# Block-sparse attention with a soft mixture of experts: probabilities turned on the vector engine, values kept on chip, all engines ordered by a planner

## The chip, the cores and the metric

The kernel runs on one core of one Trainium2 chip. The metric is the time of one execution in microseconds (us), the median of several runs; lower is better. The engines are named as in the profile: PE multiplies matrices, DVE is the vector engine, ACT the scalar engine, POOL the general engine, SP issues DMAs. Everything is float32.

## The reference, cut to what matters

```python
# q, k, v: [4 batches, 8 heads, 768 positions, 64]; blocks of 32 positions, 24 of them
scores = q @ k^T / 8
mask = |blk_i - blk_j| <= 1, or blk_i in (0, 23), or blk_j in (0, 23), or blk_j one of 3 sampled for blk_i
attn = softmax(where(mask, scores, -1e9));  x = (attn @ v) as [3072 tokens, 512]
logits = x @ phi                       # [3072, 32]: 8 experts of 4 slots each
d = softmax over tokens(logits);  c = softmax over slots(logits)
slot_input = d^T @ x                   # [32, 512]
slot_out[e] = relu(slot_input[e] @ w1[e]) @ w2[e]      # w1 [8, 512, 1024], w2 [8, 1024, 512]
out = c @ slot_out                     # [3072, 512]
```

A block of queries between 1 and 22 therefore meets eight blocks of keys: the first and the last, its own with its two neighbours, and three sampled ones (a sampled block that is there already counts once). Blocks 0 and 23 of the queries meet all keys.

## The kernel before, in words

The work of a batch is cut into units. A *sparse* unit is one block of 32 queries with all eight heads (88 of them in the four batches); a *dense* unit is a pair of heads for the query blocks 0 and 23 together (16 of them).

For a sparse unit POOL and ACT first gather 256 keys from `ktile` into a stage `kst` (`stage_k`: the fixed blocks on POOL in lines 190 and 193, the three sampled ones on ACT in line 199, with block numbers read into registers). The values of the unit are loaded from DRAM for that unit alone into a stage `vst` (`stage_v`: plain DMAs on SP and an indirect DMA issued by POOL in line 219). `do_qk` (line 306) multiplies queries with keys: a product takes the 128 rows of a pair of heads, with zeros in the queries of DRAM where the other head stands, and 64 columns of the array. `do_soft` takes the maximum on DVE (line 322) and the exponential on ACT (line 325). `do_tr` turns the probabilities with four products against an identity on PE (line 354) and copies them out of PSUM on DVE or ACT in turn (lines 335 and 337). `av_half` (line 391) multiplies with the values for four units at a time, one head to a product, 65 columns wide (the 65th holds ones and gives the sum); lines 398 to 400 divide. Dense units do the same in lines 298, 313, 319, 345 and 371.

A *tile* is 128 tokens. `moe_front` takes each of the 24 tiles through PE turns (413), logits (458, 465, 466), a running maximum, an exponential (473), and a sum over tokens into `sacc` (497, 500). After the last tile the experts run: `ffn1` (714), `ffn2` (722), and `combine` (814), which writes the result in two column halves with `store`. The expert weights come in 64 pieces of 512 KB (`load_w`, line 80); 29 have places of their own and are issued during the attention, 15 more take the place of attention buffers as these come free, and the rest follow as pieces are used up.

PE and DVE follow the order in which the program is written: the main loop runs two or three units ahead with the first products, and fixed offsets (`EOFF`) place the steps of `moe_front`. The other engines are ordered by the framework. SP carries all plain DMAs in one queue.

Of the kernel before, what the change touches and what calls it, by code (L numbers as in the profile page):

```python
# [25 lines left out]
NE, SE, FF = 8, 4, 1024  # L26
NT = S // P
VW = H * (D + 1)
VROWS = S + BLK
# [3 lines left out]
# attention: buffers, and the order of the dense (D) and first sparse (S) units of a batch  # L33
NKST, NV, NQ = 3, 8, 3
PB, PTB, XB = 4, 4, 2
SB, TB = 3, 3
VORD = [3, 2, 1, 0, 7, 6, 5, 4]
ORDER0 = "DDSDDSS"
ORDER = "DSDDDSS"
KSTEP, VLOOK, VMOST, EARLY = 5, 7, 2, 4  # L40
EVPAT = "AD"
# half steps after a tile of tokens at which the parts of its slot input come, and for the last tiles
EOFF = [3, 6, 8, 9, 11, 15]
EOFFL = [[3, 7, 9, 10, 12, 13], [3, 6, 8, 9, 11, 13]]
# experts: w2 in CS column parts, weights in pieces of WP, NPRE of them loaded during the attention
# [7 lines left out]
NPRE, NLA, NLB = 29, 3, 12  # L53
W0, W1 = 3, 3
# [3 lines left out]
MAN = {mybir.EngineType.PE, mybir.EngineType.DVE}  # L58
TMAN = MAN | {mybir.EngineType.Activation}


@with_exitstack
def attn_moe_kernel(ctx, tc, qT, kT, vtab, sampled, phi, w1, w2, out):
# [4 lines left out]
    wpre = ctx.enter_context(tc.tile_pool(name="wpre", bufs=NPRE))  # L68
    pw = ctx.enter_context(tc.tile_pool(name="pw", bufs=2))

    wsrc = [w1[e, hf] for hf in range(2) for e in range(NE)]
    wsrc += [w2[s_, g] for s_ in range(CS) for g in range(NE)]
    # the weights come in pieces of [P, WP]
# [3 lines left out]
    def load_w(m, pool):  # L77
        t = pool.tile([P, WP], F32, name=f"w{m}", tag="w")
        n, j = m // PW, m % PW
        SP.dma_start(out=t, in_=wsrc[n].rearrange("p c f -> p (c f)")[:, j * WP:(j + 1) * WP])  # L80
        wtile[m] = t.rearrange("p (c f) -> p c f", f=512 if n < 2 * NE else CW)

# [14 lines left out]
    sacc = const.tile([P, P], F32, name="sacc")  # L97
    ssum = const.tile([P, 1], F32, name="ssum")

# [1 line left out]
    NG = 96  # L101
    sreg = const.tile([1, NB, NR], I32, name="sreg")
    gidx = const.tile([NG, B, NB], I32, name="gidx")

    scr = pw.tile([P, DM], F32, tag="x", name="scr", bufs=XB)
    sraw = scr[0:NG, 0:NB * NR * 2].bitcast(I32).rearrange("p (i j w) -> p i j w", i=NB, j=NR)

    def index_load():
        SP.dma_start(
            out=sraw.rearrange("p i j w -> p (i j w)"),  # L110
            in_=sampled.bitcast(I32).rearrange("i j -> (i j)").partition_broadcast(NG),
        )
        DVE.tensor_copy(out=sreg, in_=sraw[0:1, :, :, 0])

    def index_math():
        o = NB * NR * 2
        rf = scr[0:NG, o:o + NB * NR].rearrange("p (i j) -> p i j", i=NB)
        DVE.tensor_copy(out=rf, in_=sraw[:, :, :, 0])
        o += NB * NR
        own, dup, tmp, iot, pm = (scr[0:NG, o + k * NB:o + (k + 1) * NB] for k in range(5))  # L120
        for j in range(NR):
            s_ = slice(32 * j, 32 * j + 32)
            DVE.tensor_copy(out=own[s_], in_=rf[s_, :, j])
            POOL.iota(iot[s_], pattern=[[1, NB]], base=0, channel_multiplier=0,
                      allow_small_or_imprecise_dtypes=True)
            POOL.iota(pm[s_], pattern=[[0, NB]], base=0, channel_multiplier=1,
                      allow_small_or_imprecise_dtypes=True)
# [7 lines left out]
        for j in range(1, NR):  # L135
            s_ = slice(32 * j, 32 * j + 32)
            for k in range(j):
                DVE.tensor_tensor(out=tmp[s_], in0=own[s_], in1=rf[s_, :, k], op=ALU.is_equal)
                DVE.tensor_tensor(out=dup[s_], in0=dup[s_], in1=tmp[s_], op=ALU.max)
        DVE.tensor_scalar(out=own, in0=own, scalar1=float(BLK), scalar2=None, op0=ALU.mult)  # L140
        DVE.tensor_scalar(out=tmp, in0=own, scalar1=-1.0, scalar2=float(S), op0=ALU.mult, op1=ALU.add)
        DVE.tensor_tensor(out=tmp, in0=tmp, in1=dup, op=ALU.mult)
        DVE.tensor_tensor(out=own, in0=own, in1=tmp, op=ALU.add)
        DVE.tensor_tensor(out=own, in0=own, in1=pm, op=ALU.add)
        for b in range(B):
            DVE.tensor_scalar(out=gidx[:, b, :], in0=own, scalar1=float(b * VROWS), scalar2=None,
                              op0=ALU.add)

    # ================= attention =================
# [3 lines left out]
    pk = att.enter_context(tc.tile_pool(name="pk", bufs=1))  # L153
    pst = att.enter_context(tc.tile_pool(name="pst", bufs=1))

    ktile = pk.tile([P, NP, S], F32, name="ktile")
    # but for the first, in the order in which the end of the attention frees them, the last first
    kst = [pst.tile([P, NP, 256], F32, name="kst0")]
    vst = {n: pst.tile([P, 2, VW], F32, name=f"vst{n}") for n in VORD}
    kst += [pst.tile([P, NP, 256], F32, name=f"kst{n}") for n in range(1, NKST)]  # L160
    qc = [pst.tile([P, NP, 2, 2 * BLK], F32, name=f"qc{n}") for n in range(NQ)]

    vflat = vtab.rearrange("b s w -> (b s) w")

    def load_k(b):
        for p in range(NP):
            SP.dma_start(out=ktile[:, p, :], in_=kT[b, p])

    def load_q(b, c):
        SP.dma_start(out=qc[(b * (NB // 2) + c) % NQ], in_=qT[b, c])  # L170

    def q_of(b, i):
        c = (i + 1) // 2
        return qc[(b * (NB // 2) + c) % NQ][:, :, (i + 1) % 2, :]

    # running counters of the rotating stages
    nsp = [0]      # K stages filled
    vfree = list(range(NV))
    vown = {}
    kfresh = {}    # stage -> batch whose global keys it holds  # L180
    vfresh = {}

    def stage_k(b, i):
        n = nsp[0] % NKST
        nsp[0] += 1
        st = kst[n]
        kv = ktile
        if kfresh.get(n) != b:
            kfresh[n] = b
            POOL.tensor_scalar(out=st.rearrange("p c (g s) -> p c g s", g=2)[:, :, :, 0:BLK],  # L190
                               in0=kv.rearrange("p c (g s) -> p c g s", g=NB)[:, :, 0:NB:NB - 1, :],
                               scalar1=SCALE, scalar2=1.0, op0=ALU.mult, op1=ALU.mult)
        POOL.tensor_scalar(out=st[:, :, BLK:P], in0=kv[:, :, (i - 1) * BLK:(i + 2) * BLK],  # L193
                           scalar1=SCALE, scalar2=1.0, op0=ALU.mult, op1=ALU.mult)
        _, vals = nc.values_load_multi_w_load_instructions(
            sreg[0:1, i, :], engines=[mybir.EngineType.Activation], min_val=0, max_val=NB - 1,
            skip_runtime_bounds_check_because="block numbers lie in range by the definition of the input")
        for j in range(NR):
            ACT.activation(out=st[:, :, 160 + BLK * j:192 + BLK * j],  # L199
                           in_=kv[:, :, ds(vals[j] * BLK, BLK)], func=AF.Copy, scale=SCALE)  # L200
        return st
# [77 lines left out]
    def pump_v(lim, most=99):  # L279
        while vnext[0] < min(lim, len(units)) and most > 0:  # L280
# [7 lines left out]
            else:  # L288
                if not vfree:
                    return  # L290
# [615 lines left out]
```

## Time and profile before

| | |
|---|---|
| median of 3 runs | 391.88 us (389.75 to 396.16) |
| profiled execution, first to last instruction | 410.4 us (no other time of this execution is given) |
| PE, DVE, ACT, POOL busy | 353.6, 220.0, 209.9, 142.3 us |
| moved by DMA | 105.56 MB, 257 GB/s over the span |

The profiled execution is longer than the timed ones by 18.5 us; its durations are those of that one execution. "Busy" counts the time from the start of an instruction to its end, and neighbours overlap; the time that an instruction adds to a row of like ones is therefore its distance to the next start. An instruction on PE is one of two passes of a float32 product; a turn has one.

### The profile page before, as it was taken

How to read it: one execution, taken by the hardware profiler on the slowest of the kernel's cores; microseconds unless marked ns; L12 is line 12 of the kernel's file. 1: busy time of each engine (PE TensorE's matmuls, PEld its weight loads, DVE VectorE, ACT ScalarE, POOL GpSimd, SP SyncE). 2: the span in 40 equal slices, each digit the busy share in tenths (PEclk: the TensorE clock that was granted, in tenths of full speed). 3: DMA queues.
4: the chain of work that ended last, by engine and by line, in shares of the span. 5: the costliest groups of instructions: out<-in, count | busy, mean ns of one | idle time of the engine just before them, and what ended most of it. 6: DMA issues, size and time to landing. Idle time of an engine off the chain costs nothing.

```text
span 410.4 us, 14102 instructions
## 1 busy us (share of the span) xinstructions
PE 353.6 (86%) x5525; PEld 228.1 (56%) x5525; DVE 220.0 (54%) x618; ACT 209.9 (51%) x689; POOL 142.3 (35%) x216
## 2 busy tenths in 40 slices
PE   5788988799899867998999698989989899799970
PEld 2456655467566544665665465657556556435550
DVE  3655635466455535676565356756556687501350
ACT  1655756466457625672766276638556563310350
POOL 1625425432153544234445244333453243120000
PEclk9999999899899989999999799999999899999995
DMA  7977999989859979999599759965965499899978
GB/s 242 299 221 224 312 291 246 287 272 314 214 153 286 264 237 312 292 274 286 140 271 274 244 164 277 309 173 147 265 162 138 124 242 396 308 357 410 360 248 250
DMA packets 47841, 105.56 MB, mean 257 GB/s; under 512 B 6976, under 2 KB 13856, under 8 KB 47776
## 3 DMA queue, kind: packets, MB, share of 16 engines
q1 hardware_dynamic: 42144, 87.08, 68.5%
q0 software_dynamic: 5632, 17.58, 16.4%
q8 instruction: 44, 0.72, 0.8%
q14 instruction: 21, 0.17, 0.1%
HBM read 98.34 MB, written 6.29 MB: 255 GB/s over the span
## 4 chain that ended last, share of the span: by engine, by line
PE 81%; issue 6%; DVE 3%; DMA 3%; SPq 2%; ACT 1%; POOL 1%; ACTq 0%; POOLq 0%; DVEq 0%
PE s L306 22%; PE av L391 13%; PE ps L354 12%; PE sd L298 6%; PE pso L722 4%; PE pf L714 3%; PE mxt L413 3%; PE avd L371 3%; PE psd L345 3%; PE mlt L465 2%; PE ms L497 2%; PE mlp L458 2%; DMA ktile<-in_kT_dram 2%; PE po L814 2%; DMA vst<-in_vtab_dram 1%
## 5 line engine op out<-in xcount | busy, mean ns | idle before, releaser
L219 POOL DMA_INDIRECT vst<-in_vtab_dram,gidx x88 | 83.3, 946 | 111.9 <-PE av L391 89.2
L306 PE MATMUL s<-kst,qc 128*64 128x256 f32 x704 | 100.8, 404 | 8.9 <-issue 6.3
L199 ACT ACTIVATE kst<-ktile 128x128 f32 x264 | 67.0, 312 | 56.7 <-PE ps L354 18.9
L322 DVE TENSOR_REDUCE nm<-s 128x2 f32<-128x512 f32 x88 | 60.4, 687 | 45.5 <-PE s L306 20.4
L325 ACT ACTIVATE p<-s,nm 128x256 f32<-128x256 f32 x176 | 73.9, 475 | 12.0 <-DVE nm L322 9.6
L193 POOL TENSOR_SCALAR kst<-ktile 128x384 f32<-128x384 f32 x88 | 45.3, 519 | 76.0 <-PE s L306 62.2
L391 PE MATMUL av<-vst,ptt 128*32 128x65 f32 x2816 | 59.2, 225 | 12.0 <-issue 10.9
L306 PEld LDWEIGHTS s<-kst,qc 128*64 128x64 f32 x704 | 44.7, 139 | 38.0 <-issue 19.2
L391 PEld LDWEIGHTS av<-vst,ptt 128*32 128x32 f32 x2816 | 49.2, 111 | 20.4 <-issue 17.9
L354 PE MATMUL ps<-ident,p 128*128 128x128 f32 x352 | 58.9, 291 | 0.0
L354 PEld LDWEIGHTS ps<-ident,p 128*128 128x128 f32 x352 | 38.0, 143 | 22.1 <-issue 14.0
L337 DVE COPY ptt<-ps 128x512 f32<-128x512 f32 x44 | 30.2, 685 | 34.2 <-PE av L391 22.0
L335 ACT COPY ptt<-ps 128x512 f32<-128x512 f32 x44 | 25.8, 587 | 40.3 <-PE ps L354 26.2
L319 ACT ACTIVATE pd<-sd,nb 128x384 f32<-128x384 f32 x32 | 17.7, 579 | 32.0 <-DVE nb L316 17.1
L298 PE MATMUL sd<-ktile,qc 128*128 128x384 f32 x64 | 27.9, 564 | 5.1 <-DMA ktile<-in_kT_dram 5.1
L400 DVE TENSOR_TENSOR x<-av,rs 128x256 f32<-128x256 f32 (+1 forms) x48 | 20.3, 423 | 1.6
L313 DVE TENSOR_REDUCE nm<-sd 128x1 f32<-128x384 f32 x32 | 17.1, 553 | 7.2 <-PE sd L298 4.8
L337 DVE COPY xT<-mxt 128x512 f32<-128x512 f32 (+2 forms) x25 | 16.5, 661 | 7.4 <-PE mxt L413 3.5
L345 PE MATMUL psd<-ident,pd 128*128 128x128 f32 x96 | 14.8, 293 | 5.3 <-DVE ptt L337 5.3
L298 PEld LDWEIGHTS sd<-ktile,qc 128*128 128x128 f32 x64 | 12.3, 215 | 12.4 <-DMA qc<-in_qT_dram 4.3
L371 PEld LDWEIGHTS avd<-vst,ptd 128*64 128x64 f32 x384 | 13.7, 143 | 7.0 <-DVE ptd L337 2.1
L497 PE MATMUL ms<-x,d 128*32 128x128 f32 x192 | 10.2, 285 | 8.3 <-DVE ptt L337 7.1
(110 smaller groups left out, 352.4 us busy)
## 6 DMA issues: line engine op xcount, KB each, us to landing
w<-in_w_dram SPq DMA_DIRECT2D x64, 512.0 KB
vst<-in_vtab_dram SPq DMA_DIRECT2D x80, 195.0 KB
qc<-in_qT_dram SPq DMA_DIRECT2D x47, 256.0 KB
vst<-in_vtab_dram SPq DMA_DIRECT2D x24, 260.0 KB
ktile<-in_kT_dram SPq DMA_DIRECT2D x15, 384.0 KB
out_dram<-ob SPq DMA_DIRECT2D x20, 256.0 KB
vst<-in_vtab_dram SPq DMA_DIRECT2D x72, 65.0 KB
vst<-in_vtab_dram,gidx POOLq DMA_INDIRECT x88
```

What stands on the lines that cost most here:

```text
L193: POOL.tensor_scalar(out=st[:, :, BLK:P], in0=kv[:, :, (i - 1) * BLK:(i + 2) * BLK], scalar1=SCALE, scalar2=1.0, op0=ALU.mult, op1=ALU.mult)
L199: ACT.activation(out=st[:, :, 160 + BLK * j:192 + BLK * j], in_=kv[:, :, ds(vals[j] * BLK, BLK)], func=AF.Copy, scale=SCALE)
L219: POOL.indirect_dma_start(out=st[32:128, 1, :], out_offset=None, in_=vflat, in_offset=bass.IndirectOffsetOnAxis(ap=gidx[:, b, i:i + 1], ax ...
L298: PE.matmul(u.s[n], lhsT=qc[u.b * (NB // 2) % NQ][:, u.pair].rearrange("p a c -> p (a c)"), rhs=ktile[:, u.pair, 384 * n:384 * (n + 1)], s ...
L306: PE.matmul(u.s[64 * c:64 * c + 64, hf, :], lhsT=q[:, p, :], rhs=u.kst[:, p, :], start=True, stop=True)
L322: DVE.tensor_reduce(out=nm, in_=u.s, axis=AX.X, op=ALU.max, negate=True)
L325: ACT.activation(out=u.p[:, hf, :], in_=u.s[:, hf, :], func=AF.Exp, bias=nm[:, hf:hf + 1], scale=1.0)
L337: DVE.tensor_copy(out=out, in_=in_)
L345: PE.transpose(ps[:, k, :], u.p[g][:, k * P:(k + 1) * P], ident)
L354: PE.transpose(ps[:, 2 * hf + k, :], u.p[:, hf, k * P:(k + 1) * P], ident)
L371: PE.matmul(a[64 * h2:64 * h2 + 64, u.pair, :], lhsT=u.pt[k][:, 64 * h2:64 * h2 + 64], rhs=vd[u.b][k][:, h * 65:h * 65 + 65], start=(k == ...
L391: PE.matmul(a[32 * c:32 * c + 32, hh, :], lhsT=u.pt[:, 2 * hf + k, hh * 32:hh * 32 + 32], rhs=u.vst[:, k, h * 65:h * 65 + 65], start=(k == ...
```

## The change

It is a second kernel for the same reference; the experts and the combination (lines 714 to 818) stay as they are but for the places of the weights and the order of the stores.

- **Units.** A unit is a pair of neighbouring query blocks (44 in all). A product takes 64 rows of the array (one head) and 32 columns, so that heads r = 0 and r = 1 stand on different rows and write to different PSUM banks. There are no zeros in the queries. Queries are scaled instead of keys.
- **Turning.** DVE turns the probabilities in squares of 32 by 32 from SBUF to SBUF; the products with the identity and the copies out of PSUM are gone. A head's keys of one block then lie on 32 partitions, and two heads on 64.
- **Values.** The values of a batch are loaded once into a table of 3.3 MB with two heads to 64 partitions, zeros beside each, so that one product takes two heads and 130 columns. POOL copies the three sampled blocks of each query block out of this table (`stage_v`, three copies of 260 elements with register offsets); the other blocks are read where they lie. There is no indirect DMA.
- **Front of the experts.** Four tiles go through the logits, the exponential and the sums together, each on its own 32 partitions; `sacc` has 512 columns, and four partial maxima are joined at the end.
- **Planner.** Every step is a task with engines to choose from, an assumed duration, a key and buffers. `Plan.run` orders the tasks of all five engines, which then run in that order. Loads of later batches and of weights are cut into slices of 32 partitions and held back by a rate (0.22 MB per us) and by a PE instruction that each must wait for.
- **Weights.** 26 pieces have places before the last step of the attention (11 of their own, and `ktile`, the first values table, the turned dense probabilities and the second `ktile` as these come free); 15 more follow at its end, as before.
- **Stores.** The first tiles of the four batches are combined first and stored by three DMAs for each column half instead of six.

```diff
-            for hf in range(2):
-                for c in range(2):
-                    p = 2 * hf + c
-                    PE.matmul(u.s[64 * c:64 * c + 64, hf, :], lhsT=q[:, p, :],
-                              rhs=u.kst[:, p, :], start=True, stop=True)
+            for j in range(2):
+                for p in range(NP):
+                    for r in range(2):
+                        s_ = slice(64 * r, 64 * r + 64)
+                        PE.matmul(u.s[r][32 * p:32 * p + 32, j, :], lhsT=u.q[s_, p, j, :],
+                                  rhs=kd[j][0][s_, p, :], start=True, stop=True)
...
+                DVE.transpose(out=T.pt[r][:, :, 2 * w:2 * w + 2, :].rearrange("p k j q -> p j k q"),
+                              in_=u.p[r].rearrange("p j (k q) -> p j k q", k=8))
...
+            for j in range(NR):
+                POOL.tensor_copy(out=st[:, :, j:j + 1, :], in_=vf[:, :, ds(t.vals[j], 1), :])
...
+    def av_mm(av, o, m, g, r, lhsT, rhs, start, stop):
+        PE.matmul(av[o:o + m, g, r * 2 * D1:(r + 1) * 2 * D1].rearrange("p (a d) -> p a d", a=2),
+                  lhsT=lhsT, rhs=rhs, start=start, stop=stop)
+
+    G2 = [(g, slice(64 * g, 64 * g + 64)) for g in range(2)]
...
+        for n, c in enumerate((4, 5)):
+            for r in rs_:
+                for g, s_ in G2:
+                    av_mm(T.av, 64 * r if one else 0, m, g, r, T.pt[r][s_, c, 0:m // BLK].rearrange("p j q -> p (j q)"),
+                          vt[s_, :, (0, NB - 1)[n], r, :], n == 0, False)
+        for c in (1, 2):
+            for w, u in enumerate(us):
+                for r in rs_:
+                    for g, s_ in G2:
+                        av_mm(T.av, 64 * r if one else 64 * w, 64, g, r,
+                              T.pt[r][s_, c, 2 * w:2 * w + 2].rearrange("p j q -> p (j q)"),
+                              vt[s_, :, 2 * u.g + c, r, :], False, False)
+        for n in range(NR + 1):
+            for w, u in enumerate(us):
+                for r in rs_:
+                    for j in range(2):
...
+                            av_mm(T.av, (64 * r if one else 64 * w) + 32 * j, 32, g, r, T.pt[r][s_, c, 2 * w + j], v_,
+                                  False, n == NR)
...
+                for k in range(NB):
+                    for r in range(2):
+                        for g, s_ in G2:
+                            av_mm(T.avd, 64 - 64 * r, 64, g, r, ptd[r][s_, k].rearrange("p j q -> p (j q)"), vt[s_, :, k, r, :],
+                                  k == 0, k == NB - 1)
...
-NPRE, NLA, NLB = 29, 3, 12
+NPRE, NLB = 11, 9
+KW = {"ktile": 3, "v0": 6, "v1": 6, "ptd": 3}
...
+    ORDER = [g % (B * NT // TG) for g in range(-B // TG, (B * NT - B) // TG)]
```

In the products with the values (`av_heads`, two pairs and so four query blocks at a time), the first loop takes the first and the last block of keys with 128 columns of the array (all four query blocks at once), the second a pair's own two blocks with 64 columns, the third one neighbour and the three sampled blocks with 32 columns. The last loop of the diff is the dense one: 24 blocks of keys, 64 columns.

More of the change, by code (lines that the diff above doesn't have):

```diff
@@ L163, in attn_moe_kernel @@
[L163 to L194, printed above, removed]
+    ktile, vtile = [None] * B, [None] * B
@@ L507, in diag @@
-    def diag(t, ne, n, e0=0, k0=0, nk=None):
-        a_ = t[:, 0, k0:, e0 * SE:e0 * SE + SE].copy()
-        part = a_.ap[0]
-        return bass.AP(a_.tensor, a_.offset, [list(part), [n * NS + SE, ne], [NS, nk or n], [1, SE]])
+    plan = Plan(tc, dict(s=SB, av=1, pt=MB, p=PB, ptt=PTB, kst=NKST, vrs=NVR, x=XB, xT=XTB, k=2, v=2, q=NQ,
+                     ptd=1, lp=1, dT=1, d=1), free=("pt",))
+    add = plan.add
+    class Rec:
+        pass
+    t_idx = add(lambda t: index_load(), ("ACT", 2.0), [], -40)
```

1227 lines of the change are left out of this document (757 added, 470 removed).

## The prediction

> **What bounds the kernel now.** I read the page's busy times and its chain first.
>
> ```profile
> span 410.4 us, 14102 instructions
> PE 353.6 (86%) x5525; PEld 228.1 (56%) x5525; DVE 220.0 (54%) x618; ACT 209.9 (51%) x689; POOL 142.3 (35%) x216
> DMA packets 47841, 105.56 MB, mean 257 GB/s; under 512 B 6976, under 2 KB 13856, under 8 KB 47776
> PE 81%; issue 6%; DVE 3%; DMA 3%; SPq 2%; ACT 1%; POOL 1%; ACTq 0%; POOLq 0%; DVEq 0%
> PE s L306 22%; PE av L391 13%; PE ps L354 12%; PE sd L298 6%; PE pso L722 4%; PE pf L714 3%; PE mxt L413 3%; PE avd L371 3%; PE psd L345 3%; PE mlt L465 2%; PE ms L497 2%; PE mlp L458 2%; DMA ktile<-in_kT_dram 2%; PE po L814 2%; DMA vst<-in_vtab_dram 1%
> ```
>
> PE holds 81% of the chain, and no other engine is busy for more than 54%. The lines of the attention and of the front (306, 391, 354, 298, 413, 371, 345, 465, 497, 458) make 68%, 279 us. So PE's work counts, and what it costs is the distance from one start to the next. The timeline of PE inside a batch gives it:
>
> ```profile
> 122.00 1.08 PE L306 MATMUL s<-kst,qc 128*64 128x256 f32 x8
> 123.02 0.66 PE L354 MATMUL ps<-ident,p 128*128 128x128 f32 x4
> 123.60 0.42 PE L497 MATMUL ms<-x,d 128*32 128x128 f32 x8
> 123.96 0.66 PE L413 MATMUL mxt<-ident,x 128*128 128x128 f32 x4
> 124.55 0.44 PE L306 MATMUL s<-kst,qc 128*64 128x256 f32 x2
> ...
> 131.62 1.11 PE L391 MATMUL av<-vst,ptt 128*32 128x65 f32 x64
> 132.67 0.65 PE L306 MATMUL s<-kst,qc 128*64 128x256 f32 x4
> ...
> 185.11 1.56 PE L298 MATMUL sd<-ktile,qc 128*128 128x384 f32 x4
> 186.60 0.92 PE L371 MATMUL avd<-vst,ptd 128*64 128x65 f32 x24
> 187.45 0.66 PE L354 MATMUL ps<-ident,p 128*128 128x128 f32 x4
> ```
>
> A sparse unit takes 1.02 us in 306, 0.58 in 354 and, with four units to two groups of 1.05, 0.52 in 391. Next I read the two ends.
>
> ```profile
> 13.02 1.97 PE L306 MATMUL s<-kst,qc 128*64 128x256 f32 x8 [2.12 <-ACT pd L319]
> ...
> 335.82 0.60 PE L306 MATMUL s<-kst,qc 128*64 128x256 f32 x4
> 336.46 41.15 SPq L80 DMA_DIRECT2D w<-in_w_dram  x32
> ...
> 356.22 2.78 PE L714 MATMUL pf<-w,sT 128*32 128x512 f32 x24 [0.61 <-DVE sT L682]
> 359.52 5.36 PE L714 MATMUL pf<-w,sT 128*32 128x512 f32 x48
> ...
> 360.00:390.00 30.00, 30.00 (x373) 15.26 (x366) 4.85 (x13) 5.55 (x12) 1.15 (x2) 1.00 0.99 380
> ```
>
> PE runs steadily from 13.0 us; the last first-product of the attention ends at 336.4, and there a stream of weights starts that keeps the DMA engines 99% busy at 380 GB/s (the row of the stretch 360 to 390). I therefore cut the span into 13 us of start, 323 us of loop and 74 us of tail. Some 13 us of the 279 lie outside the loop (dense products before 13.0, the last tile behind 336.4): 266 us of work in 323, or 82%.
>
> **The change part by part.** First a price. 48 instructions of 512 columns take 5.36 us on four column groups: 0.447 us for one, 0.87 ns a column. By it the four of 298, on the whole array, need 1.34 us and take 1.49; the 64 of 391, four at a time, 0.90 and take 1.05; the eight of 306, two at a time, 0.89 and take 1.02. So column groups overlap fully, and each change of form adds about 0.15 us. I take it that two row groups overlap as fully; no row shows it (below, a rival).
>
> - *Queries with keys.* A pair issues 32 instructions of 256 columns on eight places: 0.89 + 0.15 = 1.04 us, 44 times 45.8 us. Dense: 32 of 384 columns, 1.34 + 0.15, eight times 11.9 us.
> - *Turns on PE* of probabilities (0.58 us for each of 88 units, 51 us, and the dense ones) go.
> - *Values.* 130 columns are 0.113 us. For four blocks: 16 instructions on two places (0.90), 32 on four (0.90), 128 on eight (1.81), six changes of form (0.9): 4.52 us, 20 times 90 us, where 391 took 2.1 us for four. This part gets dearer: half of each product is zeros. The four single pairs take 2.1 each, 8.4; dense 192 on four places, 5.58, four times 22.3 us.
> - *Front.* 24 tiles turned at 0.59 (123.96 to 124.55) 14.2 us; logits and sums 1.04 each and two turns of about 0.3 (a quarter of 0.58 and a change of form) for six groups, 16.1 us.
>
> PE's sum is 209 us against 279, with 13 outside the loop again 196 in it. Now the other engines, DVE by its groups and by starts in a row:
>
> ```profile
> L322 DVE TENSOR_REDUCE nm<-s 128x2 f32<-128x512 f32 x88 | 60.4, 687 | 45.5 <-PE s L306 20.4 <-PE ps L354 18.4 <-ACT p L325 2.8
> L400 DVE TENSOR_TENSOR x<-av,rs 128x256 f32<-128x256 f32 x40 | 17.0, 424 | 1.3
> ```
>
> ```profile
> 125.40 0.68 DVE L337 COPY xT<-mxt 128x512 f32<-128x512 f32 x1
> 126.00 0.68 DVE L322 TENSOR_REDUCE nm<-s 128x2 f32<-128x512 f32 x1
> ```
>
> ```profile
> 23.09 1.01 DVE L313 TENSOR_REDUCE nm<-sd 128x1 f32<-128x384 f32 x2
> ```
>
> - *DVE.* 88 maxima stay, at 0.60 apart (125.40 to 126.00) 53 us. 88 turns of 512 elements are new. The nearest rows are copies and maxima of 512 elements at 0.60 to 0.69 us; below, one element in half the time would give 0.34, above, twice the copy 1.37. I take 0.64, between the copy's distance and its duration, 56 us. Dense maxima and turns 64 at 0.50, 32 us; the divisions (twice as wide as 400's 0.42, plus two small ones) about 33; the front 9 and the combination 6, copies of the turned tiles 14 where ACT doesn't take them. Together 189 to 203 us, just under PE's.
>
> POOL's largest group of copies, and POOL's and ACT's starts in a row:
>
> ```profile
> L193 POOL TENSOR_SCALAR kst<-ktile 128x384 f32<-128x384 f32 x88 | 45.3, 519 | 76.0 <-PE s L306 62.2
> ```
>
> ```profile
> 10.00 0.41 POOL L190 TENSOR_SCALAR kst<-ktile 128x256 f32<-128x256 f32 x1 [7.93 <-DMA ktile<-in_kT_dram]
> 10.36 0.52 POOL L193 TENSOR_SCALAR kst<-ktile 128x384 f32<-128x384 f32 x1
> 10.84 0.41 POOL L190 TENSOR_SCALAR kst<-ktile 128x256 f32<-128x256 f32 x1
> ```
>
> ```profile
> 15.45 0.71 ACT L199 ACTIVATE kst<-ktile 128x128 f32 x3
> 16.06 0.84 ACT L325 ACTIVATE p<-s,nm 128x256 f32<-128x256 f32 x2
> ```
>
> - *ACT.* Exponentials 88 times 0.74 to 0.84, 65 to 74; sampled keys 88 times 0.61, 54 us; dense 15; front 8: about 150.
> - *POOL.* The indirect DMA goes; three copies of 260 elements at 0.36 (10.00 to 10.36) make 1.08 us, 88 times 95 us; fixed keys 0.48, with the first ones 47; queries 48 of 256 elements, at most 18: 142 to 160 us. It is not the bound unless register offsets stop it; their cost is open, nothing to 0.3 us a block (an estimate: half of ACT's three offset copies), 26 us, which POOL's slack takes.
>
> The rows for both ends are the first 10 us, the issue of two weights and of the last six stores:
>
> ```profile
> 0.00:10.00 10.00, 4.90 (x7) 2.29 (x8) 2.93 (x12) 1.86 (x2) 1.39 (x13) 1.00 0.75 238
> ```
>
> ```profile
> 336.46 0.91 SPq L80 DMA_DIRECT2D w<-in_w_dram  x2
> ```
>
> ```profile
> 404.11 3.75 SPq L780 DMA_DIRECT2D out_dram<-ob  x6
> ```
>
> - *DMA.* Queries lose their zeros (12.3 to 6.3 MB), values come once a batch (3.3 or 1.7 MB): 62 MB in place of 105.6. At 257 GB/s that is 242 us, so nothing waits for bandwidth in the loop; SP's 270 or so issues, at 0.46 us (two in 0.91), take 125 us of it. A paced load that waits on SP holds only what is queued behind it, loads for a later batch.
> - *Start.* Before the first product with values, all keys and values of batch 0 must land: 1.6 + 3.3 MB and 0.5 MB of queries at 238 GB/s are 23 us, in which PE has 7 to 10 us of first products. That loses about 13 us, as now.
> - *Tail.* "Weights preloaded" is 26 pieces where 29 stood, so the stream behind the attention is three pieces longer: 1.6 MB at 380 GB/s, 4 us more. Three stores come in place of L780's six of 0.63 us, and earlier: 2 us less. 74 becomes 76.
>
> How well is the loop filled? Of the 57 us lost now, DMA (3%), SPq (2%) and POOL (1%) are 24 us of the chain, and their causes go: 266 of 299 would be 0.89. DVE, almost as full as PE, adds waits of its own. I take 0.88: 196 / 0.88 = 223. The sum is 13 + 223 + 76 = 312 us on the scale of the profiled execution, whose 410.4 stands at 391.88 by the timed runs, a factor 0.955: **298 us**. With 0.82 (as now) it is 314, with 0.95 283.
>
> **The rivals.**
>
> 1. *Row groups don't overlap* (slower). All products with keys or values use 64 rows; the trace has none of that kind, and only its columns show overlap. Of PE's 209 us, 179 are such products, and they would double: (196 + 179) / 0.88 + 89 = 515, 492 us. It decides from a factor of 1.49 on these 179 us, where the total reaches 410. An overlap that isn't full, halfway to that point at 1.25, is 363, 347 us. Against both: three rows give the same price a column with one, two and four column groups. The Trainium skill, "TensorE: Matmul & The Clock Gate", section Part 3, says that tiles of different rows run concurrently too and measured a factor of 3.07 for four row tiles. By 3.07 in place of 4 an estimate of the factor is 1.3 and of the time 356 us, close to the middle way; the same section's 2.38 for three column tiles is less than the full overlap that the rows here show for columns.
> 2. *POOL and DVE stop each other.* Both now work out of SBUF all the time. If every turn (72 us) held POOL up, POOL would need 160 + 72 = 232 us and set the pace: 232 in place of 209 makes 196 into 217, 336 us, 320. For it: copies of values pass straight to a waiting product. Against: POOL's copies of line 193 take 0.52 us in the quiet start (10.36) and 0.519 in the mean of all 88, beside a DVE that is busy for half of the time, though mostly from PSUM. The Trainium skill, "SBUF — State Buffer", section SBUF: two separate sides, states an exclusive lock between GpSimd and a DVE instruction that uses two ports. No run here shows whether a turn is one of those.
> 3. *DVE becomes the bound*, when a turn takes more than about 0.7 us. At 1.37, the upper end, 88 turns add 64 us and the dense ones 16: up to 203 + 80 = 283 us in place of 209, so 196 becomes 265, 390 us, 373. At 1.0 it is about 335.
> 4. *The new order stalls* on wrong durations, five queues fixed at once, so that PE loses twice the 6% of the chain that "issue" takes now, 25 us of 323 more: 0.82 becomes 0.74, 354, 338 us.
>
> **How the numbers follow.** Forecast 0.74 (280 to 316). Rows that don't overlap 0.04, the half-full overlap 0.04; POOL held up 0.06; DVE the bound 0.06; stalls 0.05; a case within 2% of before 0.01. A measurement of this kernel can tell about 2%. The range takes the forecast with its fillings (0.95 with a tail 7 us shorter gives 276), the POOL case and the stalls, 276 to 338. Faster by over 2% holds all but 0.05: 0.94; same 0.02; slower 0.04.
>
> **What would show it.** In the page after: groups of 32 first-products that start 1.04 us apart from what follows (2 us or more: rival 1); about 4.5 us of PE for a tile's values; DVE turns of about 0.65 us; no DMA_INDIRECT; 62 MB; POOL copies near 0.4 us, longer beside turns in rival 2; the chain still mostly PE, with DVE second; from the last first-product to the end about 76 us. I am wrong if the chain is mostly DVE or POOL, or if PE's distances double.

## The result, and the profile after

| | |
|---|---|
| the changed kernel | 323.46 us, median of 4 runs (320.83 to 323.69) |
| the kernel before, on the same chip | 392.38 us, median of 4 runs (389.75 to 396.16) |
| ratio | 0.8234, 95% interval 0.817 to 0.8297 |
| profiled execution of the changed kernel | 323.36 us, span 321.6 us |

Medians here and below are over all runs, while ratios leave out the runs over 1.5% above the fastest of their kernel, so that a ratio need not be that of its two medians.

The kernel is 18% faster than the one before, and 25.5 us slower than its forecast of 298. The page of the changed kernel, busy times, transfers and the shares of the chain:

```profile
span 321.6 us, 17549 instructions
PE 284.4 (88%) x7137; PEld 194.2 (60%) x7137; DVE 214.0 (67%) x492; ACT 165.2 (51%) x506; POOL 179.9 (56%) x505
DMA packets 31778, 63.61 MB, mean 198 GB/s; under 512 B 5457, under 2 KB 18898, under 8 KB 31698
PE 50%; DMA 25%; DVE 10%; issue 4%; ACT 3%; POOLq 2%; POOL 2%; SPq 1%; ACTq 1%
```

PE is busy for 69 us less than before and is still the fullest engine; DVE has come up from 54% to 67%. Of the 105.56 MB 63.61 are left, where the forecast said 62. What is new is that the chain is PE for only half of the time: DMA has 25% of it, DVE 10%. (The chain differs between executions of this same kernel: further below DMA has 12% of it in c1.) The groups of PE that replace the old products (line, form, count, busy us, mean ns, idle time before them):

```profile
L490 PE MATMUL s<-kst,q 64*32 64x256 f32 x1408 | 51.2, 380 | 5.7 <-POOL kst L419 2.2 <-issue 1.3 <-ACT p L510 1.2
...
L568 PE MATMUL avd<-v,ptd 64*64 64x130 f32 x768 | 23.4, 271 | 1.2 <-DVE x L564 0.6 <-DVE ptd L693 0.4
...
L658 PE MATMUL sd<-ktile,q 64*32 64x384 f32 x256 | 16.6, 488 | 2.0 <-ACT p L510 1.8
```

and the timeline of PE, two pairs of first products early in the loop, then the end of the attention (start, duration, form, count):

```profile
28.66 2.02 PE L490 MATMUL s<-kst,q 64*32 64x256 f32 x64
...
229.91 1.96 PE L490 MATMUL s<-kst,q 64*32 64x256 f32 x63
231.80 0.66 PE L746 MATMUL mxt<-ident,x 128*128 128x128 f32 x4
232.39 1.71 PE L568 MATMUL av<-v,ptt 64*128 64x130 f32 x40
233.89 1.27 PE L568 MATMUL av<-vrs,ptt 64*32 64x130 f32 x48
235.09 1.71 PE L568 MATMUL av<-v,ptt 64*128 64x130 f32 x40
...
259.42 3.59 PE L1090 MATMUL pf<-w,sT 128*32 128x512 f32 x16 [0.34 <-DVE tot L987]
```

Here two pairs, 64 instructions, take 2.0 us: 1.0 for a pair, as priced. The 88 instructions for half of the values of four blocks run from 232.39 to 235.09, 2.7 us here. The last first product ends at 231.9 and the experts begin at 259.4. Three stretches of the trace (start and end, then us and count of PE, PEld, DVE, ACT and POOL, the granted clock, the share of DMA and GB/s) show the whole loop, a part of it, and the stream of weights:

```profile
13.00:231.90 218.90, 206.08 (x6166) 148.80 (x6158) 178.87 (x386) 140.30 (x448) 161.37 (x456) 0.99 0.51 144
...
120.00:160.00 40.00, 39.04 (x1176) 28.17 (x1166) 36.74 (x87) 26.48 (x81) 28.94 (x83) 1.00 0.44 126
260.00:290.00 30.00, 30.00 (x320) 13.09 (x316) 5.16 (x22) 5.09 (x10) 3.52 (x6) 0.95 1.02 404
```

Over the whole loop PE is busy for 94% and DVE for 82%, with DMA at 0.51; in its fullest part, 120 to 160 us, it is 98% and 92%. Behind it DMA is the full resource, at 404 GB/s, and PE's 30.00 us hold only 320 instructions, about a third of the loop's rate. Cut as the prediction cuts it, with the start put at 13 us again, 321.6 us are 13 of start, 219 of loop and 89.7 of tail; the forecast had 13, 223 and 76.

### The profile page after: what moved, and what is told of

Its sections match the earlier page's. It is cut to its first block, busy times and chain, and to the rows that moved or that the text cites. A ratio compares the mean times of both kernels' runs of the same rounds, so it can differ in the third digit from the quotient of the medians.

```text
span 321.6 us, 17549 instructions
## 1 busy us (share of the span) xinstructions
PE 284.4 (88%) x7137; PEld 194.2 (60%) x7137; DVE 214.0 (67%) x492; ACT 165.2 (51%) x506; POOL 179.9 (56%) x505
## 2 busy tenths in 40 slices
DMA packets 31778, 63.61 MB, mean 198 GB/s; under 512 B 5457, under 2 KB 18898, under 8 KB 31698
## 4 chain that ended last, share of the span: by engine, by line
PE 50%; DMA 25%; DVE 10%; issue 4%; ACT 3%; POOLq 2%; POOL 2%; SPq 1%; ACTq 1%
PE av L568 25%; DMA w<-in_w_dram 10%; PE s L490 8%; DMA v<-in_w_dram 6%; PE avd L568 5%; DMA q<-in_qT_dram 5%; PE mxt L746 3%; PE sd L658 3%; DMA phis<-in_phi_dram 2%; DVE ptt L517 2%; DMA v<-in_vfull_dram 2%; DVE x L564 2%; PE po L1196 2%; POOLq L316 2%; ACT p L510 2%
## 5 line engine op out<-in xcount | busy, mean ns | idle before, releaser
L435 POOL COPY vrs<-v 128x260 f32 x264 | 94.7, 404 | 23.8 <-PE av L568 16.8
L568 PE MATMUL av<-v,ptt 64*64 64x130 f32 (+2 forms) x1728 | 77.0, 291 | 0.0
L517 DVE STREAM_TRANSPOSE ptt<-p 128x512 f32<-128x512 f32 x88 | 58.1, 692 | 23.7 <-ACT p L510 23.6
L568 PEld LDWEIGHTS av<-v,ptt 64*64 64x64 f32 (+2 forms) x1728 | 51.7, 134 | 24.4 <-issue 16.0
L490 PE MATMUL s<-kst,q 64*32 64x256 f32 x1408 | 51.2, 380 | 5.7 <-POOL kst L419 2.2
L411 POOL COPY kst<-ktile 128x384 f32<-128x384 f32 x88 | 43.0, 507 | 16.3 <-PE s L490 15.1
L568 PE MATMUL av<-vrs,ptt 64*32 64x130 f32 x2112 | 48.6, 281 | 3.0 <-issue 2.9
L417 ACT ACTIVATE kst<-ktile 128x128 f32 x171 | 38.9, 302 | 13.6 <-PE s L490 10.6
L490 PEld LDWEIGHTS s<-kst,q 64*32 64x32 f32 x1408 | 30.0, 106 | 18.2 <-issue 5.7
L568 PEld LDWEIGHTS av<-vrs,ptt 64*32 64x32 f32 x2112 | 36.7, 107 | 6.1 <-issue 5.6
L419 POOL COPY kst<-ktile 128x128 f32 x93 | 23.2, 293 | 1.9 <-issue 0.8
L746 PE MATMUL mxt<-ident,x 128*128 128x128 f32 x96 | 15.9, 287 | 6.4 <-DVE x L564 6.4
```

The lines of the kernel that those rows point to most:

```text
L411: POOL.tensor_copy(out=st[:, :, w:w + 96], in_=kv[:, :, (i - 1) * BLK:(i + 2) * BLK])
L417: ACT.activation(out=st[:, :, o:o + BLK], in_=src, func=AF.Copy, scale=1.0)
L419: POOL.tensor_copy(out=st[:, :, o:o + BLK], in_=src)
L435: POOL.tensor_copy(out=st[:, :, j:j + 1, :], in_=vf[:, :, ds(t.vals[j], 1), :])
L490: PE.matmul(u.s[r][32 * p:32 * p + 32, j, :], lhsT=u.q[s_, p, j, :], rhs=kd[j][0][s_, p, :], start=True, stop=True)
L517: DVE.transpose(out=T.pt[r][:, :, 2 * w:2 * w + 2, :].rearrange("p k j q -> p j k q"), in_=u.p[r].rearrange("p j (k q) -> p j k q", k=8))
```

## The experiments

Each kernel is timed beside the kernel before on its own chip. The unchanged new kernel takes 322 to 323 us wherever it ran (for the kernels b1 to b4 it did not run beside them), the kernel before 392 or 415, so variants of the new kernel are compared by their times and not by ratios across chips.

**The new kernel again (a1).** 

> The changed kernel itself, as the base of the others in this group. All theories: 323.5 us, ratio to before 0.82, with first to last instruction about 2 us below the time.

Measured: 322.04 us (321.16 to 325.12), the kernel before 415.27 (409.23 to 416.72), ratio 0.7805 (0.7706 to 0.7904). The gain depends on the chip, and it is the kernel before that varies.

**The kernel before again (a4),** unchanged, to set its profile beside its own time. 

> The kernel before, for a second profile. Theory, the profile itself lengthens this kernel (its many loads for single units and indirect DMAs), so 0.955 holds for it and not for a kernel without them: the profiled execution again spans about 410 us and the timed one about 390. Rival, the first profile caught a slow execution: the span is about 390 this time, within 2 us of the time.

Measured: the profiled execution took 419.98 us, and its page says:

```profile
span 418.1 us, 14102 instructions
```

Neither expectation held. This execution's time is its span and 1.9 us, and for every run from a1 on, of either kernel, the record has both, 1.7 to 1.9 us apart. Beside c1 the spans of the kernel before are 385.6 to 394.0 us, so recording a span does not stretch it to 410. Nor was the 410.4 us of the first profile a rare execution: all seven runs beside this one took 409 to 417 us. There are chips on which the kernel before takes 392, and others on which it takes 415. On which kind the first profile was taken is not recorded; its span fits the second.

**The kernel before without its repeated loads (b4, c4).** Values are loaded once for each place; later units work on those of the first ones, so 40 MB of loads and most indirect DMAs are left out.

```diff
     def stage_v(b, i):
...
         st = vst[n]
+        if n in vonce:
+            return st
+        vonce.add(n)
...
-                SP.dma_start(out=st[:, j, :], in_=vtab[b, (2 * k + j) * P:(2 * k + j + 1) * P, :])
+                if b == 0:
+                  SP.dma_start(out=st[:, j, :], in_=vtab[b, (2 * k + j) * P:(2 * k + j + 1) * P, :])
```

> The kernel before, with the values of each place loaded once and then kept (later blocks and batches compute with the first ones' values; some 42 MB of loads and 80 indirect DMAs are left out). Theory, PE's own work is most of what was saved, and the loads cost what the forecast gave them, 24 us of the chain: 391 us where the kernel before takes 415. Rival, nothing: 411 to 419, the waits pass to something else. Rival, the loads cost far more, and are what makes this kernel take 392 us in the first runs and 415 in later ones: 375 us or less.

> The kernel before with the values loaded once for each place (later units work on the values of the first batch). Theory: the repeated loads cost the kernel before about 42 us on any chip, a ratio of 0.88 to 0.93. Rival: the loads are what makes the kernel before take 415 rather than 392; where it takes 392 here, this one gains 25 us or less and takes 367 or more; where it takes 415, the time is 365 to 375 as in b4.

Measured: 372.78 us where the kernel before takes 415.06 (ratio 0.9092, 0.8896 to 0.9288), and 365.93 us where it takes 392.13 (0.9397, 0.9319 to 0.9475). The loads cost 42 us on the one chip and 26 on the other by the medians, about 38 and 24 by the ratios (9.1% and 6.0%). With the loads their issuing goes too: 80 of the 88 indirect DMAs, 76 us of POOL's busy time, and 153 of SP's issues. The two runs don't tell the transfers from their issuing, and "loads" stands for both below. The same stretch of the first profile of before, of b4 and of c4:

```profile
100.00:150.00 50.00, 42.70 (x664) 28.21 (x662) 26.39 (x71) 26.01 (x87) 18.99 (x27) 0.95 0.82 233
```

```profile
100.00:150.00 50.00, 50.00 (x867) 33.92 (x866) 33.21 (x87) 34.34 (x115) 8.41 (x17) 1.00 0.25 74
```

```profile
100.00:150.00 50.00, 50.00 (x938) 33.36 (x933) 33.04 (x85) 35.69 (x125) 8.42 (x17) 1.00 0.27 87
```

and the end of the loop, the last rows of first products in the timelines of b4 and of c4:

```profile
298.19 1.95 PE L312 MATMUL s<-kst,qc 128*64 128x256 f32 x16
```

```profile
288.41 1.95 PE L312 MATMUL s<-kst,qc 128*64 128x256 f32 x16
```

Without the loads PE issues 867 and 938 instructions in these 50 us in place of 664 and is never idle. The last first product ends at 300.1 in b4 and at 290.4 in c4, against 336.4 in the first profile: on chips where this kernel takes 415, as the first profile's span has it, the loads therefore cost its loop 36 us of 323, and 287 remain. The 46 us between the first profile and c4 are no price of the loads: c4 ran where the kernel before takes 392, so they hold the difference between the chips as well. So b4's rival held (375 us or less), and the 24 us that the prediction gave these waits were too few. For c4 the rival was nearer than the theory: the loads' cost is not the same on every chip. Of the 23 us between the two kinds of chip 16 lie in these loads by the medians (42 less 26), about 14 by the ratios; the other 7, between 372.78 and 365.93, are in the rest of that kernel.

**All first products on one half of the rows (b1).** Both heads of a pair take rows 0 to 63, so the second head's result is the first one's; the work is the same.

```diff
-  PE.matmul(u.s[r][32 * p:32 * p + 32, j, :], lhsT=u.q[s_, p, j, :],
-            rhs=kd[j][0][s_, p, :], start=True, stop=True)
+  PE.matmul(u.s[r][32 * p:32 * p + 32, j, :], lhsT=u.q[0:64, p, j, :],
+            rhs=kd[j][0][0:64, p, :], start=True, stop=True)
```

> In the pairs' first products both heads are taken from rows 0 to 63 of queries and keys, so that no two of them stand on different rows (head r = 1 repeats head r = 0; the dense products are as they were). Theory, the two row groups of the changed kernel overlap fully and PE paces the loop: a pair's 32 instructions take 1.93 us in place of 1.01, 44 pairs 40 us, at a fill of 0.89 45 us, 367 us. Rival, rows never overlapped: 322. Rival, another engine paces the loop and PE has room: less than 25 us more.

Measured: 340.39 us (338.8 and 341.97), 18 more than unchanged. Its timeline of PE, its loop and a part of it, and its line 490:

```profile
112.95 3.73 PE L490 MATMUL s<-kst,q 64*32 64x256 f32 x64
116.60 1.06 PE L814 MATMUL ms<-x,d 128*32 128x512 f32 x8
```

```profile
13.00:252.00 239.00, 236.96 (x6177) 175.61 (x6172) 181.18 (x390) 141.86 (x448) 165.49 (x461) 0.99 0.47 134
...
120.00:160.00 40.00, 39.99 (x1087) 31.46 (x1075) 32.90 (x74) 24.21 (x76) 26.59 (x73) 1.00 0.28 81
```

```profile
L490 PE MATMUL s<-kst,q 64*32 64x256 f32 x1408 | 87.3, 382 | 2.5 <-POOL kst L419 2.2
```

Two pairs now take 3.65 us to the next start where they took 2.0: 1.83 for one, 1.8 times as long. That the row groups of the unchanged kernel overlap is shown by undoing it. The 44 pairs cost PE 36 us more (0.83 each; line 490 is busy for 87.3 us instead of 51.2) and the kernel only 18, as the rival had it (under 25). The rest went into time that had been lost: PE is idle for 2.0 us of b1's loop where it was for 12.8 of the unchanged one (239.0 less 236.96, and 218.9 less 206.08), line 568 without the dense products takes 104 us from start to start instead of 109, and the time behind the last first product is 85.1 us instead of 89.7. That points to some 5 us of waits in line 568 that had counted as busy.

**Half of the turns done twice (b2).** The first head's probabilities are turned two times; 44 instructions are added on DVE.

```diff
   DVE.transpose(out=T.pt[r]..., in_=u.p[r]...)
+  if r == 0:
+      DVE.transpose(out=T.pt[r]..., in_=u.p[r]...)
```

> DVE turns the probabilities of head row r = 0 of every pair twice (44 turns more, 0.65 us each, 28.6 us of DVE). Theory, PE paces the loop and DVE stands a little below it: of the 28.6 us some 5 to 12 show, 327 to 334 us. Rival, DVE paces the loop as much as PE: nearly all of it, 346 to 351 us. Rival, DVE has room: under 2 us.

Measured: 334.75 us (332.63 and 336.88), 12.7 more, for 28.6 us of DVE; the theory's 327 to 334 but for 1 us. Busy times and chain of this kernel:

```profile
PE 282.4 (85%) x7137; PEld 192.5 (58%) x7137; DVE 242.7 (73%) x536; ACT 165.8 (50%) x506; POOL 180.0 (54%) x505
DVE 34%; PE 32%; DMA 17%; ACT 7%; issue 4%; SPq 2%; ACTq 2%; POOL 0%; POOLq 0%; DVEq 0%
```

DVE now leads the chain, and PE is idle for 22 us of the loop instead of 12.8. The addition to PE cost half of itself, the one to DVE 0.44 of itself (from two runs each): both engines hold the loop. Whether DVE does by its load, or by the 0.65 us that a second turn puts ahead of a pair's products with values, b2 does not tell.

**A third of POOL's copies of values (b3).** One of the three sampled blocks is copied and stands for all three.

```diff
-            for j in range(NR):
+            for j in range(1):
                 POOL.tensor_copy(out=st[:, :, j:j + 1, :], in_=vf[:, :, ds(t.vals[j], 1), :])
...
-                                v_ = u.vst[j][s_, :, n - 1, r, :]
+                                v_ = u.vst[j][s_, :, 0, r, :]
```

> POOL copies one of the three sampled blocks of values for each query block, and the products read it three times (two sampled blocks are left out); the register loads stay. 176 copies at 0.36 us, 63 us of POOL, go. Theory, POOL is off the path: within 5 us of 322. Rival, POOL's copies hold up the products with values, in steps that the chain gives to others: 10 to 20 us less, 302 to 312 us.

Measured: 322.37 us (317.72 to 323.72); POOL is busy for 121.8 us instead of 179.9 and the time stays where it was. These copies are not on the path.

**Keys' places ahead of the values' (a2).** The allocation of `kst` and `vrs` in SBUF is swapped, so that the late weights overlap places that come free at another time.

```diff
-    vrs = [pst.tile(..., name=f"vrs{n}") for n in range(NVR)]
     kst = [pst.tile(..., name=f"kst{n}") for n in range(NKST)]
+    vrs = [pst.tile(..., name=f"vrs{n}") for n in range(NVR)]
```

> Only the places of two buffers are exchanged: the key stages lie where the first weight pieces behind the attention go, so four of these wait for the last first-product (231.9 us) and no longer for the last product with values (247.9 us). Theory, the tail is a stream of weights that DMA alone paces, and it starts too late: four pieces of 0.52 MB at 405 GB/s come out of it, 5.2 us less, 318 us. Rival, the tail is as long as the chain of steps behind the last product (PE, the last stores), and the stream is hidden: 323.5, within 1 us.

Measured: 319.65 us (315.62 to 321.2), 2.4 less than a1, between the theory's 318 and the rival's 323.5. Against the same runs of the kernel before the ratios are 0.7694 (0.7534 to 0.7855) and a1's 0.7805 (0.7706 to 0.7904), whose intervals overlap, so a2 alone shows no gain. The issue of the weights by SP in the unchanged kernel, and then in a2:

```profile
231.01 7.67 SPq L198 DMA_DIRECT2D kw<-in_w_dram  x12
...
247.90 6.08 SPq L198 DMA_DIRECT2D w<-in_w_dram  x9
254.94 7.03 SPq L198 DMA_DIRECT2D v<-in_w_dram  x6
```

```profile
232.40 7.27 SPq L198 DMA_DIRECT2D kw<-in_w_dram  x12
239.77 15.00 SPq L198 DMA_DIRECT2D w<-in_w_dram  x9
254.81 6.07 SPq L198 DMA_DIRECT2D v<-in_w_dram  x6
```

and how long SP's weights waited for line 568 in the whole run, again in both (us in total, times, the longest):

```profile
SPq L198 <- PE av L568: 12.1, 4, 9.2
```

```profile
SPq L198 <- PE av L568: 14.6, 8, 8.9
```

In the unchanged kernel SP waits from 238.7 to 247.9: the first of the nine late pieces lies over `vrs`, which the last products with values read, and all weights behind it in the queue wait too. After the swap two of the nine, not four, are issued before 241 us, 8 us earlier; the third waits for 8.9 us on the same products with values, so that the nine are spread over 15.0 us in place of 6.1 and `v` follows at 254.81, about when it did (254.94). The wait moved two pieces down the queue. From the end of the last first product a2 takes 85.8 us (233.6 to 319.4), a1 87.6 (235.7 to 323.3).

**More places for queries (a3).** Eight instead of four, loaded four units earlier; one preloaded weight is given up for them.

```diff
-NKST, NVR, NQ = 4, 6, 4
+NKST, NVR, NQ = 4, 6, 8
-NPRE, NLB = 11, 9
+NPRE, NLB = 10, 9
-        t_q = add(load, ..., n - 6 if n > 2 else -30, acq=[("q", use)], byte=131072)
+        t_q = add(load, ..., n - 10 if n > 2 else -30, acq=[("q", use)], byte=131072)
```

> Eight places for queries in place of four, asked for four units earlier; one weight piece less has a place before the tail (1.3 us more there). Theory, the loop loses the 15 us that the chain gives to loads of queries, because a load is issued only a few us ahead of its product: 10 to 13 us less net, about 312 us. Rival, PE is so full that a wait for queries only moves work about: no gain in the loop, 324 to 325 us.

Measured: 319.75 us (319.27 to 327.96), 2.3 less than a1. The forecast from the chain was 10 to 13, the rival's was 324 to 325; the ratio, 0.7756 (0.7619 to 0.7893), overlaps a1's.

**Both together (c2), and the pacing taken off (c3).** c2 is a2 and a3 in one. In c3 the loads no longer wait for a PE instruction; their places in SP's queue are as before.

```diff
-            elif t.pace:
+            elif False:
```

> The changed kernel as it is, the measure for the three beside it. Both theories: 320 to 326 us, whatever the kernel before takes on this chip (392 or 415).

> Twice as many places for the queries, loaded four units earlier, and the places of the keys ahead of those of the values. Theory: PE waits less for queries in the loop (about 4 us) and the late weights start earlier (about 2 us), and the two add: 315 to 318, 4 to 7 us below the kernel as it is. Rival: what a2 and a3 gained was spread between executions, or the one eats the other's gain: 320 to 324.

> The loads of later batches and of weights are no longer held back by the rate; they still wait for their places and each for the step that it was given. Theory (pacing orders loads that nobody waits for yet, DMA is busy for under half of the loop): 320 to 326, no change. Rival (pacing keeps the loads of queries from queueing behind weights): the chain shows more DMA on queries and the time is 330 or more.

Measured on one chip, with the kernel before at 392.13: unchanged (c1) 322.22 us (321.14 to 326.15), ratio 0.8264 (0.8211 to 0.8318); both (c2) 317.52 (314.66 to 321.34), ratio 0.812 (0.806 to 0.818); without pacing (c3) 322.67 (321.53 to 324.2). The chains of c1 and of c2, by engine:

```profile
PE 54%; DVE 13%; DMA 12%; ACT 6%; issue 4%; POOL 2%; POOLq 2%; ACTq 2%; SPq 1%; DVEq 0%
```

```profile
PE 74%; DVE 10%; DMA 4%; ACT 3%; issue 3%; SPq 2%; ACTq 1%; DVEq 0%
```

The two edits add to 4.7 us, and the intervals of the two ratios do not meet: c2, at 317.5 us, is the best kernel found, 1.5% under the change itself, and its theory held (315 to 318). DMA falls from 12% of the chain to 4%, PE rises to 74%. A share of the chain is not what its removal is worth: PE took over most of these places, and the unchanged kernel, with the same time, has DMA at 25% of its chain in its first profile and at 12% here. For c1 and c3 the theories held: pacing is worth nothing that was measured (0.45 us more without it).

## Why the prediction was right, and where it was off

The forecast, 298, and the result, 323.46, are 25.5 us apart. Three terms make it up: the conversion from the profile to the timed runs 14.1 us (312 to 298), the sum itself 9.6 (312 to a span of 321.6), and 1.8 between the span and the time of an execution. The measured time lies in the recorded range, 276 to 338, but above the forecast's own, 280 to 316: the range holds it because the POOL case and the stalls had widened it, and neither of these is what made the time longer. That part was luck. Of the signs named, the 1.0 us of a pair, the turns of 0.66 us, the missing indirect DMA, the bytes and POOL's copies came; the chain that should be mostly PE with DVE second, and the tail of 76 us, did not.

**The factor 0.955 failed.** The prediction scaled its sum by 391.88 / 410.4. a4 shows that a profiled execution takes its span and 1.9 us, so there was nothing to scale within one execution; the two numbers belong to different conditions of the kernel before. And the slower condition is for about two thirds a matter of its repeated loads (42 us on one chip, 26 on the other), which the change removes: it takes 322 us beside a kernel before of 415 (a1) and beside one of 392 (c1). The factor was applied to a kernel that no longer has what it describes. 312 and 1.8 would have been 314.

**The tail was 13.7 us too short.** "74 becomes 76" took the stream of weights to start at the last first product, as the row at 336.46 shows for before. It started at 247.9, 16 us behind the last first product. From there to the end are 73.7 us, as from 336.4 to the end before. So the length of the stream was right and its start was not. The other runs agree: in b1 and b2 the stream starts at 265.5 and 260.0 us, and the spans end 71.5 and 70.8 us later. Two things hold it: two tiles' products with values are still to come behind the last first product (232.4 to 249.3), and SP's next weight waits for them (the rows of SP above). a2 shows that changing the places lets two pieces through and leaves the others waiting for the same products; the time behind its last first product is 2 us shorter than a1's (85.8 and 87.6).

**The loop was right within 4 us, by two errors that cancel.** PE's price a column held wherever the products follow each other freely: 1.0 us a pair against 1.04 priced, 2.9 us for a unit of dense products with values against 2.8 (23.1 of 22.3 in all). Elsewhere the same instructions take longer (dense first products twice, then half of the values of four blocks to the next start):

```profile
124.10 2.99 PE L658 MATMUL sd<-ktile,q 64*32 64x384 f32 x32
...
132.25 1.52 PE L658 MATMUL sd<-ktile,q 64*32 64x384 f32 x31
...
150.32 1.71 PE L568 MATMUL av<-v,ptt 64*128 64x130 f32 x40
151.82 0.92 PE L568 MATMUL av<-vrs,ptt 64*32 64x130 f32 x48
152.49 1.16 PE L490 MATMUL s<-kst,q 64*32 64x256 f32 x32
```

Dense first products, priced at 1.49 us, take 1.5 us at 132.25 (31 of the 32) and 2.9 at 124.10; the 88 instructions priced at 2.26 us take 2.17 at 150.32 and 2.7 at 232.39. From each start to the next, less the idle time that the profile shows, line 490 takes 48.5 us against 45.8, line 658 15.9 against 11.9, and line 568 without the dense ones 109 against 98.4. So the excess is not in the columns. Part of it is, by b1, waiting that the profile counts as busy (5 us of line 568); what holds the rest isn't shown.

PE is busy for 206 us of the loop, 0.94 of it, but that can't be set beside the forecast's 0.88, which divides priced work by the loop. The kernel before, filled to 0.82 by that measure, has PE busy for 289.7 of its 323.4 us, or 0.90:

```profile
13.00:336.40 323.40, 289.74 (x4674) 191.57 (x4674) 188.74 (x514) 187.00 (x630) 130.18 (x182) 0.97 0.85 240
```

By the forecast's measure the new loop is filled to 196 / 219 = 0.895. Inside it two errors cancel. The loads' waits were taken as 24 us of 57, and b4 shows 36: without them the old loop would be filled to 266 / 287 = 0.93 and not to 0.89. And for the new kernel's own waits, DVE's above all, the step from 0.89 to 0.88 allowed some 3 us, where 0.93 to 0.895 is 8. That b2 costs time fits this; no run takes these waits apart.

**DVE as forecast.** The turn and the maximum:

```profile
L517 DVE STREAM_TRANSPOSE ptt<-p 128x512 f32<-128x512 f32 x88 | 58.1, 692 | 23.7 <-ACT p L510 23.6
L505 DVE TENSOR_REDUCE nm<-s 128x2 f32<-128x512 f32 x88 | 54.7, 677 | 1.5 <-PE s L490 1.3
```

58.1 us for the 88 turns, 0.66 each against 0.64 taken, between the bounds of 0.34 and 1.37. The sum, 214.0, is 11 us above the upper end. DVE is not the bound alone (rival 3), but b2 shows that more of it costs time. ACT's 165.2 us is 15 above its about 150.

**POOL was more, and it did not matter.** Its groups, and the register loads behind its offsets (count: ns min/median/max, first and last start):

```profile
L435 POOL COPY vrs<-v 128x260 f32 x264 | 94.7, 404 | 23.8 <-PE av L568 16.8
L411 POOL COPY kst<-ktile 128x384 f32<-128x384 f32 x88 | 43.0, 507 | 16.3 <-PE s L490 15.1
...
L419 POOL COPY kst<-ktile 128x128 f32 x93 | 23.2, 293 | 1.9 <-issue 0.8
```

```profile
L316 POOLq TENSOR_LOAD <-vreg x88: 722/728/752, 13.7 to 240.8; - x88
L316 ACTq TENSOR_LOAD <-sreg x57: 687/702/900, 2.2 to 224.2; - x57
L316 POOLq TENSOR_LOAD <-sreg x31: 722/728/936, 8.9 to 223.9; - x31
```

The copies of values are 94.7 us, the 95 of the prediction. The sum, 179.9 us, is 20 above its upper end, as the planner gave POOL sampled keys too (line 419, 23.2 us) that the prediction had put on ACT. A load of registers takes 0.73 us on POOL and stands in no busy sum: 88 of them are 64 us in POOL's queue, where the open term held 26, and 31 more for the sampled keys make it 87. b3, which keeps these loads and takes 58 us of copies away for no gain, shows that POOL has room for them.

**The rivals.** *Rows that don't overlap* is refuted by the 1.0 us of a pair, and by b1, where one row group makes it 1.83. Each of these rows holds two pairs and one change of form; less 0.15 us for that they are 1.85 and 3.50 us, a factor of 1.89 of 2. The Trainium skill, "TensorE: Matmul & The Clock Gate", section Part 3, says that tiles of different rows run concurrently, which the runs confirm; its 3.07 for four row tiles is further from full than what two show here. *POOL and DVE stop each other* is refuted: copies of line 411 that spend over half of their time beside a turn take 505 ns (18 of them), those beside none 507 (61), and turns take 694 ns beside POOL's work and 690 without it. (Line 193, which moved as many elements and scaled them, took 519 before there were any turns.) The lock that the Trainium skill, "SBUF — State Buffer", section SBUF: two separate sides, describes for two-port instructions is not seen beside this turn. *The new order stalls* is not seen at its 25 us: POOLq, SPq and ACTq are 4% of the chain, and c2, which changes places and the order of loads, finds 4.7 us.

**One sentence of the prediction was wrong in kind:** that a paced load on SP holds only loads for later batches. Loads of queries stand in the same queue, and the new kernel's chain contains four of them (91.30 is one, behind pieces of `ktile`):

```profile
39.38 3.49 DMA q<-in_qT_dram
50.24 3.85 DMA q<-in_qT_dram
91.30 3.63 DMA q<-in_qT_dram
212.50 4.19 DMA q<-in_qT_dram
```

Its price is small (2.3 us in a3, within the spread), and taking the wait for a PE instruction off these loads gains nothing (c3).

So the gain comes in two parts, by the spans of the first profiles, 88.8 us in all: the loop goes from 323 to 287 us without the repeated loads (b4) and from there to 219; the tail gives 15.7 us of it back. By the times it is 69 us here, as this chip's kernel before takes 392. That the 68 us from 287 to 219 come from less work on PE is the prediction's sum (196 us priced for 266) and not an experiment: no run separates the turns on DVE, the values kept on chip and the new order. What stays open besides: why the kernel before takes 392 us on one chip and 415 on another, in its loads and beyond them; what holds the rows of products that take longer than their price; and what a tail would take in which no late weight waits for a place.

## What to carry to other kernels

Before converting a sum from a profile to timed runs, ask what makes the two differ and whether the change removes it: here a factor of 0.955 belonged for about two thirds to loads that were to go. Find the one transfer behind the last step whose place is still being read, since a single queue lets everything wait behind it, and place late data over what comes free first, and look at the second place too. Two engines at 94% and 82% of a loop can share it: here work added to either showed by about half, and a share of the chain overstated what its removal brought. Compare a fill only with one counted in the same way.

## What the runs showed of the hardware that was not expected

- The kernel that moves 105.56 MB varies between chips (392 us on two occasions, 415 on two others), while the one that moves 63.61 MB took 322 to 323 us on the three occasions when it ran beside it. Without 40 MB of the loads the first varies by 7 us (365.93 and 372.78).
- Two groups of 64 rows overlap by a factor of 1.8, together with four groups of columns (1.0 us against 1.83 a pair).
- A load of a register list from SBUF takes 0.70 to 0.73 us on ACT and POOL, longer than one of the three copies of 260 elements that it serves on POOL (0.404).
- DVE turns 128x512 elements of float32 in squares of 32 in 692 ns, about as long as its maximum over as many (677), and POOL's copies are not slower beside it (505 and 507 ns).
